# VectorE rounds the fill's operands with one-element maxima in place of copies, and the turning of -max and 1/sum moves one step later

## The chip, the cores and the metric

The kernel runs on one core of a Trainium2 chip. The metric is device time in microseconds (us), from launch to end, of one execution. A core has TensorE (PE, matmuls; PEld is its weight loading), VectorE (DVE), ScalarE (ACT), GpSimd (POOL) and SyncE (SP, which here only issues DMAs). Each engine takes its instructions strictly in the order in which they were written.

## The reference

Two independent parts, written side by side into one output of 2048 x 2048 (float32):

```python
q = (x @ wq)  -> 32 heads of 32;  k = x @ wk;  v = x @ wv     # one k, v for all heads; S = 2048, D = 1024
p = softmax(q k^T / sqrt(32));  A = concat_heads(p v) @ wo
a = xb @ hid_re^T;  b = xb @ hid_im^T                          # DFT over the hidden axis
B = seq_re @ a - seq_im @ b                                    # DFT over the sequence, real part
out = concat([A, B], axis=-1)
```

## The kernel before

**Two streams on TensorE.** The *attention* stream goes through 32 units (4 blocks of 512 queries x 8 groups of 4 heads), 32 steps to a unit, 1024 steps in all. The *fill* is every other matrix product of the kernel (q, k, v, both DFT stages, the output product), cut into groups of 128x128 by 128x512 matmuls. A fill product is made of three matmuls, high x high, high x low and low x high parts, because each operand is split into a part `hi`, rounded to float32r, and the rest `lo`. The loop over n (L753 to L766) issues one attention step and then `level` (L745) inserts as many fill matmuls as keep the fill even; in each eighth step it inserts none, since there `pv` (L674) issues 16 small matmuls of p v for each of four heads together.

**A step of attention.** `scores` (L602) has PE write a 128x1024 tile `pss` of scores (two matmuls) and DVE take its negated row maximum into `nm` (L610). `row_sums` (L613), one step behind, has ACT take exp of that tile with the maximum as bias, and its row sum into `ls`. `expo` (L665) has PE write the transposed scores `pst` of a unit that lies 44 steps back, and ACT exponentiate them into `p`. There are two buffers of `pss` and one of `pst`, so PE's next matmul into one of them waits for ACT.

**Between the two passes of a unit** the maxima and sums must be turned from columns into rows. `score_step` (L703) does it in pieces, by the number e of the step behind the unit's end: `lse_1` (e = 1), `lse_1b` (2), `lse_2` (3), all on small tiles; `lse_3` (L643, e = 5) fills up a fill group by up to five matmuls if it is near its start or end (`aside`, L378), has PE transpose -max (high and low part) and 1/sum together (`m2`, with `ident`) into a PSUM bank `psb`, and DVE copy the result to `mt`; `lse_4` (L653, e = 7) has SP send the two -max rows into the operand `qst` (two DMAs) and 1/sum to DRAM (one DMA). The transposed scores of the unit, which need these rows of `qst`, begin at e = 12. `pv` comes at e = 4, 12, 20 and 28, after that step's `score_step`. The fill's open group, the transposes and `pv` share two banks `psb` (`bank`, L328); DVE adds each `pv` result to `ov` (L685), which frees its bank.

**How a fill operand is made** (`Line`, L139): SP loads the float32 source (`r` for right operands, `m` for left ones), POOL adds further sources to it where the product needs sums (`comb`, L211), `cast` (L174) writes `hi` (`rh`, `mh`; called at L225 and L235), and `lo` (L244) has POOL write the difference (`rl`, `ml`). Each piece is issued a fixed number of fill matmuls ahead of need. `cast` is done by ACT before the fill position START (L572) and by DVE behind it. The small `CAST`s of `oh` and of `m` are other lines (L700, L638).

Of the kernel before, what the change touches and what calls it, by code (L numbers as in the profile page):

```python
# [11 lines left out]
ALU = mybir.AluOpType  # L12
AX = mybir.AxisListType
# [74 lines left out]
def tile_kernel(ctx: ExitStack, tc, xT, wq, wkv, wo, xbT, wT, cT, out):  # L88
# [3 lines left out]
    dve = Ordered(tc, nc.vector)  # L92
# [4 lines left out]
    def pool(stack, name, bufs, **kw):  # L97
        kw.setdefault("reuse_waits", "tile")
        return stack.enter_context(tc.tile_pool(name=name, bufs=bufs, **kw))
# [32 lines left out]
    op = pool(ctx, "op", 2, side="right")  # L132
# [41 lines left out]
    def cast(to, of):  # L174
        if pos["fill"] < START:
            act.activation(to, of, AF.Copy)
        else:
            dve.tensor_copy(to, of)

    def load_r(it):  # L180
        if it.pre or it.t:
# [37 lines left out]
    def hi_r(it):  # L219
        it.hi = rp.tile([P, W], F32R, name="rh")  # L220
        it.lo = rp.tile([P, W], F32R, name="rl")
        if it.pre:
            fetch(it)
        else:
            cast(it.hi, it.t[0])  # L225

    def hi_m(it):
        it.hi = mp.tile([P, 4, P], F32R, name="mh")
        it.lo = mp.tile([P, 4, P], F32R, name="ml")
        if it.pre:  # L230
            fetch(it)
            return
        _, n, w = it.t[0].shape
        it.hi, it.lo = it.hi[:, :n, :w], it.lo[:, :n, :w]
        cast(it.hi, it.t[0])  # L235
# [355 lines left out]
    def open_unit(u):  # L591
        b, g = units[u]
        assert ("q", b, g) in ready
        q = qsp.tile([P, 4, W], F32R, name="qst")
        gp.memset(q[96:P].bitcast(F32), 0.0)
        for r, src in enumerate((qh_d, ql_d, qh_d)):
            move(sp, q[r * DH:(r + 1) * DH], src[b][g].rearrange("(h d) c -> d h c", d=DH))
        qst[u] = q
        nm[u] = sm.tile([P, 2, NC], F32, name="nm")
        ls[u] = sm.tile([P, 2, NC], F32, name="ls")  # L600

    def scores(s):  # L602
        u, r = divmod(s, SU)
        i, j = divmod(r, 2)
        h, t = divmod(i, 4)
        ps = ps_s.tile([P, 2 * W], F32, name="pss")
        for a in range(2):
            k0 = (2 * j + a) * W
            te.matmul(ps[:, a * W:(a + 1) * W], qst[u][:, h, t * P:(t + 1) * P], kst[:, k0:k0 + W], start=True, stop=True)
        dve.tensor_reduce(nm[u][:, j, i:i + 1], ps, axis=AX.X, op=ALU.max, negate=True)  # L610
        pend[s] = ps

    def row_sums(s):  # L613
        if s not in pend:
            return
        ps = pend.pop(s)
        u, r = divmod(s, SU)
        i, j = divmod(r, 2)
        act.activation(ps, ps, AF.Exp, bias=nm[u][:, j, i:i + 1], accum_out=ls[u][:, j, i:i + 1])

    def lse_1(u):
        m = sm.tile([P, NC], F32, name="mm")
        d = sm.tile([P, 2, NC], F32, name="md")
        dve.tensor_tensor(m, nm[u][:, 0], nm[u][:, 1], op=ALU.min)
        for j in range(2):
            dve.tensor_sub(d[:, j], m, nm[u][:, j])
        lse[u] = m, d

    def lse_1b(u):
        act.activation(lse[u][1], lse[u][1], AF.Exp)  # L630

    def lse_2(u):
        m, d = lse[u]
        l = sm.tile([P, NC], F32, name="l")
        m2 = sm.tile([P, 3, NC], F32, name="m2")
        dve.tensor_mul(d, d, ls[u])
        dve.tensor_add(l, d[:, 0], d[:, 1])
        dve.tensor_copy(m2[:, 0].bitcast(F32R), m)  # L638
        dve.tensor_sub(m2[:, 1], m, m2[:, 0])
        dve.reciprocal(m2[:, 2], l)  # L640
        lse[u] = m2

    def lse_3(u):  # L643
        m2 = lse.pop(u)
        aside()
        pm = bank("psb")
        te.transpose(pm[:3 * NC, :P], m2.rearrange("p a b -> p (a b)"), ident)
        mt = sm.tile([3 * NC, P], F32, name="mt")
        dve.tensor_copy(mt, pm[:3 * NC, :P])
        cur["at"] += 1  # L650
        lse[u] = mt

    def lse_4(u):  # L653
        mt = lse.pop(u)
        for a in range(2):
            move(sp, qst[u][96 + a:97 + a].rearrange("o h (t c) -> o (h t) c", c=P), mt[a * NC:(a + 1) * NC])
        sp.dma_start(r_d[u], mt[2 * NC:])
# [45 lines left out]
    def score_step(s):  # L703

        if s < total:
            u, r = divmod(s, SU)
            if r == SU - 6 and u + 1 < len(units):
                open_unit(u + 1)
            scores(s)
        row_sums(s - 1)  # L710
        u, e = divmod(s - SU, SU)
        if 0 <= u < len(units):
            if e == 1:
                lse_1(u)
            elif e == 2:
                lse_1b(u)
            elif e == 3:
                lse_2(u)
            elif e == 5:
                lse_3(u)  # L720
            elif e == 7:
                lse_4(u)


# [11 lines left out]
    for s in range(SU + LEAD):  # L736
        score_step(s)
        take(7)
# [14 lines left out]
    for n in range(total):  # L753
        u, r = divmod(n, SU)
        if n == total - 12:
            w1 = wo_set(1)
            add([o_group(NQ - 1, t, e, ws) for e, ws in ((0, w0), (1, w1)) for t in range(4)])
        score_step(n + SU + LEAD)
        if ends:
            ends.pop(0)()  # L760
        expo(n)
        if r == 16:
            inverse(u)
        if r % 8 == 0 and n:
            pv(*divmod(n // 8 - 1, 4))
        level(n)  # L766
# [72 lines left out]
```

## Time and profile before

| what | value |
|---|---|
| median of 3 runs (lowest to highest) | 2849.58 us (2846.28 to 2852.26) |
| the profiled execution's own time | 2849.53 us |
| its span, first to last instruction | 2847.8 us |
| granted TensorE clock, mean | 0.997 |
| busy PE, ACT, DVE, POOL | 98%, 77%, 68%, 43% of the span |

The profiled execution's time is 1.7 us over its span, and 0.05 us under the median of the runs. In the profile's lines, a group is `line engine operation out<-in shapes xcount | busy us, mean ns of one | idle time just before them <- what ended it`. Nearly every instruction passes through one helper, so the line is L66 throughout and tiles tell the groups apart. The ends of matmuls are modelled: in the trace a 128x512 matmul lasts 0.39 us while the next one starts 0.23 us after it, so a PE that shows as busy can still be waiting a little.

### The profile page before, as it was taken

Reading aid. Unit: us, or ns where it says so; the run is one execution under the profiler, and the core shown is the slowest. Engines: PE = TensorE matmul, PEld = TensorE weight load, DVE = VectorE, ACT = ScalarE, POOL = GpSimd, SP = SyncE. Lnnn points to the kernel's source line nnn. Section 1 sums busy time; section 2 is a strip of 40 time slices with the busy share of each in tenths; the row PEclk is TensorE's granted clock in tenths of the full one; section 3 lists DMA queues with packets and bytes.
Section 4 is the critical chain, followed back from the end, with each engine's and each line's share of the span. In section 5 each row is a group of like instructions: output and inputs, shape, how many; then the busy total and the mean of one; then the engine's idle time right before and its main releaser. Section 6 shows DMA issues by size and latency. Waiting matters only on the chain.

```text
span 2847.8 us, 39945 instructions
## 1 busy us (share of the span) xinstructions
PE 2794.1 (98%) x13904; PEld 1929.8 (68%) x13904; DVE 1948.0 (68%) x2430; ACT 2185.7 (77%) x3151; POOL 1212.5 (43%) x928
## 2 busy tenths in 40 slices
PE   7999999999999999999999999999999999999999
PEld 5776676767666767676767666666666666667656
DVE  6876677777777777776777677677777676766511
ACT  4578788878787888888888888778788788888740
POOL 1211123454324346555664455766666753520000
PEclk9999999999999999999999999999999999999999
DMA  8865425765576455554552454654555533554445
GB/s 295 294 198 172 149 101 167 237 213 197 193 233 212 163 178 160 154 169 123 170 175 93 134 156 133 200 172 138 176 167 155 174 113 100 160 155 138 126 141 170
DMA packets 315722, 480.83 MB, mean 169 GB/s; under 512 B 33408, under 2 KB 98432, under 8 KB 315520
## 3 DMA queue, kind: packets, MB, share of 16 engines
q1 hardware_dynamic: 315520, 478.28, 52.8%
q8 instruction: 109, 1.79, 0.3%
q14 instruction: 93, 0.76, 0.1%
HBM read 364.12 MB, written 112.98 MB: 168 GB/s over the span
## 4 chain that ended last, share of the span: by engine, by line
PE 83%; DVE 7%; ACT 3%; DMA 3%; issue 2%; POOL 1%; SPq 1%; POOLq 0%; ACTq 0%; DVEq 0%
PE psb L66 53%; PE pss L66 15%; PE pst L66 15%; DVE nm L66 2%; ACT pss L66 1%; ACT p L66 1%; DMA ql<-ql 1%; DVE mh L66 1%; DVE rh L66 1%; DVE ov L66 1%; SPq L66 1%; POOL m L66 0%; DMA r<-s 0%; POOL ml L66 0%; DVE md L66 0%
## 5 line engine op out<-in xcount | busy, mean ns | idle before, releaser
L66 DVE TENSOR_REDUCE nm<-pss 128x1 f32<-128x1024 f32 x1024 | 1248.5, 1221 | 379.4 <-PE pss L66 376.6
L66 ACT ACTIVATE p<-pst 128x1024 f32<-128x1024 f32 x1024 | 1051.9, 1027 | 429.4 <-PE pst L66 426.5
L66 ACT ACTIVATE pss<-pss,nm 128x1024 f32<-128x1024 f32 x1024 | 1113.9, 1088 | 149.1 <-DVE nm L66 142.2
L66 PE MATMUL psb<-rh,mh 128*128 128x512 f32 (+1 forms) x1852 | 731.6, 395 | 12.0 <-ACT rh L66 8.2
L66 PE MATMUL psb<-rh,ml 128*128 128x512 f32 (+1 forms) x1852 | 731.9, 395 | 0.7 <-POOL ml L66 0.7
L66 PE MATMUL psb<-rl,mh 128*128 128x512 f32 (+1 forms) x1852 | 729.9, 394 | 0.3 <-DVE rl L66 0.3
L66 PE MATMUL pss<-kst,qst 128*128 128x512 f32 x2048 | 658.6, 403 | 17.2 <-ACT pss L66 16.6
L66 PE MATMUL pst<-qst,kst 128*128 128x512 f32 x2048 | 659.7, 403 | 10.2 <-ACT p L66 9.2
L66 POOL TENSOR_TENSOR rl<-r,rh 128x512 fp32r<-128x512 f32 x214 | 281.9, 1318 | 736.3 <-DVE rh L66 537.8
L66 POOL TENSOR_TENSOR ml<-m,mh 128x512 fp32r<-128x512 f32 x292 | 383.8, 1315 | 484.4 <-DVE mh L66 247.0
L66 PEld LDWEIGHTS pss<-kst,qst 128*128 128x128 f32 x2048 | 373.0, 188 | 208.2 <-issue 93.9
L66 PE MATMUL psb<-p,v 128*32 128x512 f32 x4096 | 466.5, 596 | 0.6 <-DVE h L66 0.5
L66 PEld LDWEIGHTS pst<-qst,kst 128*128 128x128 f32 x2048 | 372.7, 189 | 136.2 <-ACT p L66 54.5
L66 PEld LDWEIGHTS psb<-rh,mh 128*128 128x128 f32 (+1 forms) x1852 | 347.6, 188 | 97.5 <-ACT rh L66 8.7
L66 PEld LDWEIGHTS psb<-rh,ml 128*128 128x128 f32 (+1 forms) x1852 | 347.6, 188 | 84.1 <-POOL ml L66 1.1
L66 PEld LDWEIGHTS psb<-rl,mh 128*128 128x128 f32 (+1 forms) x1852 | 347.3, 188 | 84.5 <-DVE rl L66 1.6
L66 PEld LDWEIGHTS psb<-p,v 128*32 128x32 f32 x4096 | 120.2, 110 | 277.3 <-issue 258.0
L66 POOL TENSOR_TENSOR m<-m,m 128x512 f32<-128x512 f32 x192 | 252.6, 1316 | 13.2 <-DMA m<-in_cT_dram 7.8
L66 DVE TENSOR_TENSOR ov<-ov,psb 128x512 f32<-128x512 f32 x96 | 66.0, 688 | 265.9 <-PE psb L66 265.7
L66 POOL TENSOR_TENSOR r<-r,r 128x512 f32<-128x512 f32 x112 | 149.0, 1331 | 199.1 <-DMA r<-in_wT_dram 101.7
L66 ACT ACTIVATION_READ_ACCUMULATOR pss<-pss,nm 128x1 f32 x1024 | 208.6, 204 | 0.0
L66 DVE CAST mh<-m 128x512 fp32r<-128x512 f32 x291 | 167.1, 574 | 17.5 <-POOL m L66 10.6
(68 smaller groups left out, 848.6 us busy)
## 6 DMA issues: line engine op xcount, KB each, us to landing
m<-in_cT_dram SPq DMA_DIRECT2D x384, 256.0 KB, 3.7
r<-s SPq DMA_DIRECT2D x192, 256.0 KB, 4.3
y<-y SPq DMA_DIRECT2D x96, 256.0 KB, 4.4
r<-in_wT_dram SPq DMA_DIRECT2D x80, 256.0 KB, 3.8
m<-in_xbT_dram SPq DMA_DIRECT2D x80, 256.0 KB, 4.2
y<-u SPq DMA_DIRECT2D x80, 256.0 KB, 2.9
qst<-qh SPq DMA_DIRECT2D x64, 256.0 KB, 5.5
s<-y SPq DMA_DIRECT2D x64, 256.0 KB, 3.5
```

The lines of the kernel that those rows point to most:

```text
L66: return lambda *a, **k: self.tc.keep_in_program_order(f(*a, **k))
```

## The change

`cast` on DVE, behind START, becomes a maximum over a last axis of one element, with the same 128x512 numbers in and out; the output type float32r does the rounding as before. The condition of L175 and ACT's branch stay. `lse_3` goes from e = 5 to e = 6, `lse_4` from e = 7 to e = 8.

```diff
         if pos["fill"] < START:
             act.activation(to, of, AF.Copy)
         else:
-            dve.tensor_copy(to, of)
+            dve.tensor_reduce(to.rearrange('p a b -> p (a b)').unsqueeze(2) if len(to.shape) == 3 else to.unsqueeze(2), of.rearrange('p a b -> p (a b)').unsqueeze(2) if len(to.shape) == 3 else of.unsqueeze(2), axis=AX.X, op=ALU.max)
...
                 lse_2(u)
-            elif e == 5:
+            elif e == 6:
                 lse_3(u)
-            elif e == 7:
+            elif e == 8:
                 lse_4(u)
```

## The prediction

> **What bounds the kernel now.** I read the page first: engines, then the chain of work that ended last.
>
> ```profile
> span 2847.8 us, 39945 instructions
> PE 2794.1 (98%) x13904; PEld 1929.8 (68%) x13904; DVE 1948.0 (68%) x2430; ACT 2185.7 (77%) x3151; POOL 1212.5 (43%) x928
> PE 83%; DVE 7%; ACT 3%; DMA 3%; issue 2%; POOL 1%; SPq 1%; POOLq 0%; ACTq 0%; DVEq 0%
> ```
>
> PE is the bound. No matmul is added or taken away, so only what PE loses by waiting can change: 53.7 us show as idle (2847.8 - 2794.1). Next the waits, longest totals of PE and of what feeds it (us, times, longest).
>
> ```profile
> ACT pss L66 <- DVE nm L66: 142.2, 129, 20.0
> PEld pst L66 <- ACT p L66: 54.5, 127, 1.9
> PEld pss L66 <- ACT pss L66: 36.8, 44, 4.7
> PE pss L66 <- ACT pss L66: 16.6, 13, 4.2
> PEld psb L66 <- DVE ov L66: 13.7, 22, 1.6
> PE pst L66 <- ACT p L66: 9.2, 34, 1.5
> ```
>
> ACT waits for DVE's row maximum `nm`, and PE then waits for ACT to give back a score tile. Behind that stands the rounding on DVE. First its groups of the view by line and shape (count | busy us, mean ns of one | idle before), with an ordinary DVE subtraction of the same size and one of its lse_1 operations beside it; then, from the views by tile, the durations (min/median/max, ns).
>
> ```profile
> L66 DVE CAST mh<-m 128x512 fp32r<-128x512 f32 x291 | 167.1, 574 | 17.5 <-POOL m L66 10.6
> L66 DVE CAST rh<-r 128x512 fp32r<-128x512 f32 x214 | 123.1, 575 | 24.6 <-PE pss L66 14.6 <-DMA r<-in_wo_dram 7.2 <-DMA r<-in_xT_dram 2.9
> L66 DVE TENSOR_REDUCE nm<-pss 128x1 f32<-128x1024 f32 x1024 | 1248.5, 1221 | 379.4 <-PE pss L66 376.6
> L66 DVE TENSOR_TENSOR rl<-h,rh 128x512 fp32r<-128x512 f32 x8 | 5.0, 672 | 0.0
> L66 DVE COPY h<-psb 128x512 f32<-128x512 f32 x56 | 38.3, 684 | 3.4 <-PE psb L66 3.3
> ```
>
> ```profile
> L66 DVE CAST mh<-m x291: 355/419/1542, 47.9 to 2493.4; 128x512 fp32r<-128x512 f32 x146
> L66 DVE CAST rh<-r x214: 362/419/2110, 51.2 to 2813.2; 128x512 fp32r<-128x512 f32 x107
> L66 DVE TENSOR_REDUCE nm<-pss x1024: 1155/1225/1229, 65.6 to 2689.8; 128x1 f32<-128x1024 f32 x171
> L66 DVE TENSOR_TENSOR md<-mm,nm x64: 159/174/1323, 141.3 to 2692.3; 128x16 f32<-128x16 f32 x64
> ```
>
> A cast takes 419 ns at the median, yet 574 on average, and up to 2110. The same 512 elements cannot need that. What a long one is doing is seen in the timeline (start us, us, what; in brackets the idle time before it), for DVE, POOL, ACT and PE in turn.
>
> ```profile
> 1811.14 1.50 DVE L66 CAST mh<-m 128x512 fp32r<-128x512 f32 x1 [0.99 <-POOL m L66]
> 1812.57 1.52 DVE L66 CAST rh<-r 128x512 fp32r<-128x512 f32 x1
> 1814.00 2.34 DVE L66 TENSOR_REDUCE nm<-pss 128x1 f32<-128x1024 f32 x2
> ```
>
> ```profile
> 1811.07 1.29 POOL L66 TENSOR_TENSOR ml<-m,mh 128x512 fp32r<-128x512 f32 x1
> 1812.32 1.48 POOL L66 TENSOR_TENSOR r<-r,r 128x512 f32<-128x512 f32 x1
> ```
>
> ```profile
> 1815.31 1.09 ACT L66 ACTIVATE pss<-pss,nm 128x1024 f32<-128x1024 f32 x1 [2.80 <-DVE nm L66]
> ```
>
> ```profile
> 1814.06 0.39 PE L66 MATMUL psb<-rh,mh 128*128 128x512 f32 x1
> 1814.28 0.39 PE L66 MATMUL psb<-rl,mh 128*128 128x512 f32 x1
> 1816.57 0.73 PE L66 MATMUL pss<-kst,qst 128*128 128x512 f32 x2 [1.90 <-ACT pss L66]
> ```
>
> Each cast began just after a POOL operation had begun and ended 0.3 us after it: 1811.07 + 1.29 = 1812.36 against 1812.64, 1812.32 + 1.48 = 1813.80 against 1814.09. So a cast that finds POOL at work is held until POOL is done. Two holds in a row, DVE 2.2 us late, ACT idle 2.80 us, PE idle 1.90. The row maximum, which reads PSUM, is never held (1229 at most).
>
> **The change part by part: the rounding.** What it removes: the holds, 291 x (574 - 419) + 214 x (575 - 419) ns = 45 + 33 = 78 us of DVE. What it adds: a slower operation. No row has a maximum over single elements, out of SBUF and with 512 results. From below it costs what an unheld cast does, 0.419 us; from above what the 1024-element maximum does, 1.221 us, if every result took two cycles. The nearest rows, 512 elements in one pass on DVE, say 0.672 and 0.684; I take 0.68. DVE then has 505 x (0.68 - 0.574) = 53 us more to do, 2001 us of 2848, 70%.
>
> What the holds cost PE now: by the waits above it idles 16.6 + 9.2 = 25.8 us for ACT. A matmul's end is modelled 0.16 us late (0.39 long, the next about 0.23 later), so each of the 127 + 44 waits that the weight loads show hides up to 0.16 more: 27 us. Together some 53. In the quoted case the change moves DVE from 1814.09 to 1811.14 + 2 x 0.68 - 0.07 = 1812.43 (neighbours on DVE overlap by 0.07: 1811.14 + 1.50 against 1812.57), 1.65 us earlier, and gives PE 1.65 of its 1.90 + 0.16, 80%; the rest is DVE's wait for POOL's sum `m`, which stays. Not all waits have a cast behind them: lse_1's operations with two SBUF inputs are held as well (`md`: median 174, up to 1323 ns) and remain so. I put the casts' part at six tenths. 53 x 0.8 x 0.6 = **26 us gained** (bounds: 0 and 53).
>
> The Trainium skill, "SBUF — State Buffer", section "Who interferes with whom", tells of such a hold as an exclusive port pair shared by VectorE and GpSimd: copies and casts in a two-port mode take it for a whole instruction, and tensor_reduce on trn2 never does. The quoted holds agree with the first half; of the second the trace shows only maxima out of PSUM. By the page the gain above stands; if an SBUF-reading maximum were held like a cast, the sum would be that of the third rival.
>
> What the longer unheld cast costs: between two maxima of a light step DVE has little room.
>
> ```profile
> 1301.07 1.23 DVE L66 TENSOR_REDUCE nm<-pss 128x1 f32<-128x1024 f32 x1 [0.19 <-PE pss L66]
> 1303.16 1.23 DVE L66 TENSOR_REDUCE nm<-pss 128x1 f32<-128x1024 f32 x1 [0.86 <-PE pss L66]
> 1301.54 1.03 ACT L66 ACTIVATE p<-pst 128x1024 f32<-128x1024 f32 x1
> 1302.46 1.09 ACT L66 ACTIVATE pss<-pss,nm 128x1024 f32<-128x1024 f32 x1
> 1302.96 0.63 PE L66 MATMUL pst<-qst,kst 128*128 128x512 f32 x2
> ```
>
> The room is 1303.16 - 1302.30 = 0.86 us. One cast of 0.68 fits; two end 2 x 0.68 - 0.07 - 0.86 = 0.43 late. ACT has 0.16 of slack behind the maximum (1302.30 to 1302.46), PE 0.39 behind ACT (1302.57 to 1302.96), so a pair is absorbed (0.43 < 0.55), and only a pair beside a third DVE operation reaches PE. There is a cast in half of the 1024 steps on average; if every second `rh` fell beside an `mh`, 107 pairs, ACT would be late by 107 x 0.27 = 29 us in all, of which I let a tenth through: **3 us lost** (bounds 0 and 29). POOL's `lo` starts 0.26 us later behind an unheld cast; its lead of several fill matmuls hides that.
>
> **The turning.** `lse_3` comes in the step right behind a `pv`, and its transposes take the bank that `pv` has just used. PE, PEld and DVE of one such step, by the timeline:
>
> ```profile
> 2043.22 0.73 PE L66 MATMUL pss<-kst,qst 128*128 128x512 f32 x2
> 2044.10 0.29 PE L66 MATMUL psb<-ident,m 128*48 128x128 f32 x1
> ```
>
> ```profile
> 2044.09 0.10 PEld L66 LDWEIGHTS psb<-ident,m 128*48 128x48 f32 x1 [0.58 <-DVE ov L66]
> ```
>
> ```profile
> 2043.36 0.69 DVE L66 TENSOR_TENSOR ov<-ov,psb 128x512 f32<-128x512 f32 x1
> ```
>
> The addition ends at 2044.05 and the transpose follows. The second `pss` matmul starts by 2043.56 (it is 0.39 long, ending 2043.95, for the usual form), so the gap is 0.54 where 0.23 would do: 0.31 us, in 22 waits, **7 us gained** (bounds: 0, and the 13.7 us that the weight loads show). One step later, over 2 us on, the addition is long done. `aside` and the copy to `mt` move along: the same matmuls in another order, and a copy behind a maximum as before. What could be late next is `lse_4`: its three DMAs leave SP a step later. In this unit:
>
> ```profile
> 2045.43 1.16 SPq L66 DMA_DIRECT2D qst<-mt  x2
> 2060.36 0.73 PE L66 MATMUL pst<-qst,kst 128*128 128x512 f32 x2 [0.18 <-ACT p L66]
> DMA to landing us min/median/max: 1.6/1.8/3.2
> ```
>
> From issue to the first use are 14.9 us; both rows have landed by 0.58 + 3.2 = 3.8 at worst. A step less (2.1 to 2.9 us) leaves 8 us: nothing on PE's path. Queued behind them on SP are loads due many matmuls later, and 1/sum is read only 16 steps into the next pass.
>
> **Sum**, against the profiled execution's own 2849.5 us (2847.8 span and 1.7 around it; the median of the runs is the same): -26 + 3 - 7 = -30, **2820 us**, 1.1% less. With the choices a third off either way: 2806 to 2834.
>
> **Rivals.**
> 1. *More comes back.* POOL's operation beside a held cast took 1.48 in place of 1.29 us; without holds POOL's sums, on which casts wait, are earlier too, and eight tenths of all 53 us return: 2849.5 - 42 - 7 = 2800. For it: DVE's idle 0.99 us for POOL in the quoted hold. Against: lse_1's holds stay.
> 2. *The holds were covered.* ACT is 77% busy, and what DVE loses ACT might make up before PE asks; then only the turning counts: 2849.5 - 7 = 2842.5. Against: PE's own 1.90 us in the quoted case.
> 3. *The lost rate decides, slower.* The maximum runs at one element a cycle, and is held or not held without PE's waits changing; the pairs make ACT late, and ACT, not PE, sets the light steps, which at 2.09 us (1301.07 to 1303.16) just hold its 1.09 + 1.03. All 29 us arrive: 2849.5 - 7 + 29 = 2871. It decides as soon as a pair ends more than 0.16 us past the room of 0.86. Against: ACT idles 23% of the span. The Trainium skill, "VectorE: DVE Perf Modes", section "Rules for kernel authors", warns of just this: a tensor_reduce runs at the base rate and is the slowest operation, where a float32 copy within SBUF runs at twice it; its fixed 150 cycles would make (512 + 150) / 0.96 = 690 ns, an estimate from that page. By that alone nothing would be gained; the trace's 574 ns average says that the doubled rate is mostly lost already.
> 4. *Single-element maxima take two cycles, slower.* At 1.22 us a lone cast is 1.22 - 0.07 - 0.86 = 0.29 late, absorbed; a pair is 1.51 late, 0.96 past ACT's and PE's slack, x 107 = 103: 2849.5 - 26 - 7 + 103 = 2920. It decides from about 0.9 us for one, where the 107 pairs eat the 33 us. For it: no row excludes it. Against: every other 512-element row is under 0.70.
> 5. *The rows of `qst` land late:* PE waiting at each unit's start; with 8 us to spare hardly.
>
> **How the numbers follow.** Forecast 0.56, rival 1 0.12, rival 2 0.14, rival 3 0.08, rival 4 0.08, rival 5 0.02. A measurement of this kernel can tell about 0.2% (5.7 us) from no change; rival 2 lies at that edge and is halved. Faster: 0.56 + 0.12 + 0.07 = 0.75; same 0.07; slower 0.18. The range reaches from rival 1's 2800, with 4 us for its own spread, over rival 2 and up to 2858, and leaves out the rest of the slower cases.
>
> **What would show it.** A group of 505 maxima `mh`, `rh` near 0.68 us, minimum and maximum close together; the 419 ns CASTs gone; ACT's wait for `nm` down from 142 towards 80 us; PE's idle 53.7 us towards 35; POOL's mean durations lower; PEld's wait for `ov` near 0; no wait of PE for `qst<-mt`. Wrong would be: maxima above 0.9 us, or held ones; ACT's wait for `nm` as long as now; a new wait at the transposes.

## The result, and the profile after

The changed kernel takes 2841.81 us (median of 8 runs, 2840.23 to 2843.98), the kernel before 2850.27 in the same measurement (8 runs, 2846.28 to 2853.23). The ratio is 0.9972, 95% interval 0.9961 to 0.9983: faster by 8 us, not by the 30 that were forecast. Differences in us below are differences of such ratios times 2850; each ratio has about 0.0012 to either side, so a difference between two kernels is good to some 5 us.

The page of the changed kernel: span, engines, and the chain that ended last by engine.

```profile
span 2838.8 us, 39953 instructions
PE 2789.2 (98%) x13904; PEld 1926.1 (68%) x13904; DVE 1993.5 (70%) x2430; ACT 2184.6 (77%) x3151; POOL 1191.7 (42%) x928
PE 80%; DVE 7%; DMA 3%; issue 3%; POOL 2%; ACT 2%; SPq 1%; POOLq 0%; ACTq 0%; DVEq 0%
```

DVE has 45.5 us more to do, POOL 21 less. PE's idle is 2838.8 - 2789.2 = 49.6 us, where 53.7 were before and 35 were expected. The roundings themselves came out as forecast, by shape and by tile (last the minimum, median and maximum in ns):

```profile
L66 DVE TENSOR_REDUCE mh<-m 128x512 fp32r<-128x512 f32 x291 | 196.4, 675 | 24.4 <-POOL m L66 16.4 <-DMA m<-in_wq_dram 7.0 <-DMA wq<-mh 0.9
L66 DVE TENSOR_REDUCE rh<-r 128x512 fp32r<-128x512 f32 x214 | 144.5, 675 | 25.8 <-PE pss L66 14.3 <-DMA r<-in_wo_dram 7.6 <-DMA r<-in_xT_dram 2.0
```

```profile
L66 DVE TENSOR_REDUCE mh<-m x291: 622/676/689, 48.1 to 2484.9; 128x512 fp32r<-128x512 f32 x146
```

0.675 us on average, never above 0.689: nothing holds them. What that does is seen at a pair of roundings that was held in the kernel before, in the same way as the pair that the prediction quotes. There, on DVE, ACT and PE:

```profile
2260.48 1.49 DVE L66 CAST mh<-m 128x512 fp32r<-128x512 f32 x1 [0.95 <-POOL m L66]
2263.33 2.34 DVE L66 TENSOR_REDUCE nm<-pss 128x1 f32<-128x1024 f32 x2
2264.64 1.09 ACT L66 ACTIVATE pss<-pss,nm 128x1024 f32<-128x1024 f32 x1 [2.75 <-DVE nm L66]
2265.89 0.78 PE L66 MATMUL pss<-kst,qst 128*128 128x512 f32 x2 [1.84 <-ACT pss L66]
```

The same pair in the changed kernel, on DVE, POOL, ACT and PE (`mh` waits 0.95 us for POOL's sum as before, `rh` follows):

```profile
2255.41 0.69 DVE L66 TENSOR_REDUCE mh<-m 128x512 fp32r<-128x512 f32 x1 [0.95 <-POOL m L66]
2256.01 0.68 DVE L66 TENSOR_REDUCE rh<-r 128x512 fp32r<-128x512 f32 x1
2256.60 2.35 DVE L66 TENSOR_REDUCE nm<-pss 128x1 f32<-128x1024 f32 x2
```

```profile
2255.33 1.30 POOL L66 TENSOR_TENSOR ml<-m,mh 128x512 fp32r<-128x512 f32 x1
2256.58 1.30 POOL L66 TENSOR_TENSOR r<-r,r 128x512 f32<-128x512 f32 x1
```

```profile
2257.91 1.09 ACT L66 ACTIVATE pss<-pss,nm 128x1024 f32<-128x1024 f32 x1 [0.87 <-DVE nm L66]
```

```profile
2259.17 0.73 PE L66 MATMUL pss<-kst,qst 128*128 128x512 f32 x2
2260.09 0.73 PE L66 MATMUL pst<-qst,kst 128*128 128x512 f32 x2 [0.18 <-ACT p L66]
```

POOL works through beside DVE. From the first rounding to the first maximum are 2256.60 - 2255.41 = 1.19 us, against 2263.33 - 2260.48 = 2.85 before; ACT waits 0.87 in place of 2.75 us, PE 0.18 in place of 1.84. In this place the working of the prediction holds. The pair that the prediction itself quotes came out otherwise. In the changed kernel it begins here (DVE, POOL, ACT):

```profile
1816.62 0.69 DVE L66 TENSOR_REDUCE mh<-m 128x512 fp32r<-128x512 f32 x1 [2.43 <-POOL m L66]
1812.30 3.04 POOL L66 TENSOR_TENSOR y<-y,h 128x512 f32<-128x512 f32 x2 [5.38 <-DMA r<-s]
1818.53 1.09 ACT L66 ACTIVATE pss<-pss,nm 128x1024 f32<-128x1024 f32 x1 [2.35 <-DVE nm L66]
```

No hold is left, but DVE waits 2.43 us for POOL's sum `m`, which stands behind two other sums, and ACT 2.35 in place of 2.80 us. (With the copies kept and the turning moved, in e1 below, DVE waits 2.43 us at this pair too, so the maximum did not bring this wait.) The waits as a whole hardly moved:

```profile
DVE nm L66 <- PE pss L66: 328.4, 513, 2.0
ACT pss L66 <- DVE nm L66: 138.5, 146, 20.6
PEld pst L66 <- ACT p L66: 58.8, 146, 2.0
PEld pss L66 <- ACT pss L66: 32.3, 47, 4.7
PE pss L66 <- ACT pss L66: 10.1, 12, 4.3
PE pst L66 <- ACT p L66: 9.6, 33, 1.6
PE psb L66 <- DVE ql L66: 4.3, 3, 1.6
PE psb L66 <- DVE h L66: 4.2, 4, 1.1
```

ACT still waits 138.5 us for the row maximum (142.2 before), now 146 times in place of 129: fewer long waits, more short ones. Three rows of before, to set beside the first and the last two:

```profile
DVE nm L66 <- PE pss L66: 376.6, 576, 1.9
PE psb L66 <- DVE ql L66: 2.4, 2, 2.0
PE psb L66 <- DVE h L66: 0.5, 1, 0.5
```

The list counts waits of over 0.15 us. In 576 of 1024 steps DVE stood idle that long until PE had the scores; in most of the other 448 it was still busy with something else when they came. With the longer roundings there are 513 and 511. The last two rows, in which PE's fill groups wait for DVE to empty a bank, have grown from 2.9 to 8.5 us.

### The profile page after: what moved, and what is told of

Read it like the earlier page. It is cut to its first block, busy times and chain, and to the rows that moved or that the text cites. A ratio compares the mean times of both kernels' runs of the same rounds, so it can differ in the third digit from the quotient of the medians.

```text
span 2838.8 us, 39953 instructions
## 1 busy us (share of the span) xinstructions
PE 2789.2 (98%) x13904; PEld 1926.1 (68%) x13904; DVE 1993.5 (70%) x2430; ACT 2184.6 (77%) x3151; POOL 1191.7 (42%) x928
## 4 chain that ended last, share of the span: by engine, by line
PE 80%; DVE 7%; DMA 3%; issue 3%; POOL 2%; ACT 2%; SPq 1%; POOLq 0%; ACTq 0%; DVEq 0%
PE psb L66 51%; PE pss L66 15%; PE pst L66 14%; DVE nm L66 3%; ACT pss L66 1%; ACT p L66 1%; DMA r<-s 1%; POOL ml L66 1%; POOL m L66 1%; SPq L66 1%; DVE mh L66 1%; DVE rh L66 0%; DMA m<-in_cT_dram 0%; DVE md L66 0%; POOL rl L66 0%
## 5 line engine op out<-in xcount | busy, mean ns | idle before, releaser
L66 ACT ACTIVATE pss<-pss,nm 128x1024 f32<-128x1024 f32 x1024 | 1113.5, 1087 | 145.8 <-DVE nm L66 138.5
L66 PE MATMUL pss<-kst,qst 128*128 128x512 f32 x2048 | 658.6, 402 | 10.4 <-ACT pss L66 10.1
L66 POOL TENSOR_TENSOR ml<-m,mh 128x512 fp32r<-128x512 f32 x292 | 377.3, 1293 | 509.4 <-DVE mh L66 247.6
L66 PEld LDWEIGHTS pst<-qst,kst 128*128 128x128 f32 x2048 | 369.9, 188 | 142.2 <-ACT p L66 58.8
L66 DVE TENSOR_REDUCE mh<-m 128x512 fp32r<-128x512 f32 x291 | 196.4, 675 | 24.4 <-POOL m L66 16.4
```

The costliest lines, as they stand in the source:

```text
L66: return lambda *a, **k: self.tc.keep_in_program_order(f(*a, **k))
```

## The experiments

Four kernels take the change apart. Theory A: the holds were worth what the prediction says, and the length of the unheld rounding ate it. Its rivals are in the texts on record. All go on from the changed kernel, which turns at e = 6 and 8.

**e1, the turning alone.**

```diff
-            dve.tensor_reduce(...)      # the one-element maximum
+            dve.tensor_copy(to, of)
```

> The copies stay, only the turning moves one step later. Theory A (the turning gave its 7 us, and in the rounding the longer maxima ate what the vanished holds gave): about 2842.5 us, 0.9974 of before, no PEld wait for ov at the transposes, holds as before. Rival B (the turning's gain was lost again by the reordered matmuls, and the rounding gave the whole): 2850, ratio 1.000. Rival C (both parts gain, the forecast's way, at half size): about 2846.

2845.73 us, ratio 0.9986 (0.9978 to 0.9995): 4 us gained, as rival C says. **e2, the maxima alone.**

```diff
-            elif e == 6:   # lse_3
+            elif e == 5:
-            elif e == 8:   # lse_4
+            elif e == 7:
```

> Maxima in place of the copies, the turning where it was. Theory A: about 2849.5, within 0.1% of before, since 78 us of holds go and 505 x 0.256 = 129 us of length come. Rival B: about 2842. Rival C: about 2846.

2844.83 us, ratio 0.9981 (0.9972 to 0.9990): 5.4 us, rival C again. The parts add up (9.4 against 8), and theory A's "nothing from the rounding" is wrong by these 5 us. **e3, as long as the maximum, but held like the copy**, since it reads two operands from SBUF.

```diff
-            dve.tensor_reduce(...)
+            dve.tensor_tensor(to, of, of, op=ALU.max)
```

> The rounding as a maximum of the source with itself, two SBUF inputs, turning moved: as long as the one-element maximum when free (0.675 us), but held by POOL as the copy is. It prices the holds alone, against the changed kernel. Theory A: holds are worth about 20 us or more, so 2862 or above. Rival D (holds never reached PE, they were covered): 2842, as the changed kernel, although its DVE operations show means near 0.83 us.

2870.29 us, ratio 1.0073 (1.0061 to 1.0086). The groups by shape and two waits of this kernel:

```profile
L66 DVE TENSOR_TENSOR mh<-m 128x512 fp32r<-128x512 f32 x291 | 251.8, 865 | 22.3 <-POOL m L66 13.2 <-DMA m<-in_wq_dram 9.1
L66 DVE TENSOR_TENSOR rh<-r 128x512 fp32r<-128x512 f32 x214 | 175.2, 819 | 24.1 <-PE pss L66 14.3 <-DMA r<-in_wo_dram 6.8 <-PE psb L66 1.7
```

```profile
ACT pss L66 <- DVE nm L66: 190.0, 176, 20.9
PE pss L66 <- ACT pss L66: 26.7, 30, 3.8
```

Above 675 ns it is held 291 x 190 + 214 x 144 ns = 86 us, much as the copy was (78). Against e1 it differs by the length of a free rounding, 1.0073 - 0.9986 = 0.0087, **25 us for the length**; against the changed kernel by the holds, 1.0073 - 0.9972 = 0.0101, **29 us for the holds**. Both take the way over `nm`, ACT and `pss`: ACT's wait is 190 us. Rival D is out. Each price was taken beside the other, though: the 25 us are the length of a rounding that is held as well, the 29 us the holds of one that is already long. A short rounding that nothing holds was not run. **e4, the length alone**, doubled by reading each element twice.

```diff
-            dve.tensor_reduce(t.unsqueeze(2), o.unsqueeze(2), ...)
+            dve.tensor_reduce(t.unsqueeze(2), o.unsqueeze(2).to_broadcast([P, W, 2]), ...)
```

> A maximum over two copies of each element (a stride of zero), turning moved: no holds, 1.21 us in place of 0.675. It prices the length alone. Theory A: length is dear once a second operation stands between two row maxima; 0.54 us more on 505 roundings cost at least as much per us as the first 0.256 did (about 20 us), so 2880 or above. Rival D (DVE has room): under 2850.

2942.42 us, ratio 1.0322 (1.0307 to 1.0336): 0.0350, 100 us more than the changed kernel. One group and one wait:

```profile
L66 DVE TENSOR_REDUCE mh<-m 128x512 fp32r<-128x1024 f32 x291 | 351.4, 1208 | 17.9 <-POOL m L66 12.0 <-DMA m<-in_wq_dram 4.2 <-POOL ml L66 1.4
```

```profile
DVE nm L66 <- PE pss L66: 218.4, 300, 2.0
```

505 x (1.208 - 0.675) = 269 us of DVE cost 100 of PE, 0.37 each, and no hold is in play (none takes over 1.223 us); the first 505 x 0.256 = 129 us, beside the holds of e3, cost 25, 0.19 each. Length is not free in either range. DVE now waits for the scores in only 300 of 1024 steps.

The next four ask which lateness of DVE counts. **e5, the maximum only for operands that POOL has summed.**

```diff
-    def cast(to, of):
+    def cast(to, of, summed):            # called with len(it.srcs) > 1
...
-        else:
+        elif not summed:
+            dve.tensor_copy(to, of)
+        else:
```

> The changed kernel, but operands with a single source are copied again and only those that POOL has summed go through the maximum. The first four runs priced the holds at about 29 us and the length at about 25. Theory A (a hold strikes a rounding that waits for POOL's sum, since POOL goes straight on to its next operation; so these have most of the holds, and the single-source ones only pay for the length): faster than the changed kernel, about 2835. Rival F (holds strike whatever comes while POOL is busy, and POOL is busy in the same stretches): no gain, 2842 to 2848.

2839.10 us, ratio 0.9961 (0.9947 to 0.9975), 3 us below the changed kernel: inside the uncertainty, so neither theory is told apart. **e6, fewer small operations that POOL can hold.**

```diff
-        dve.tensor_tensor(m, nm[u][:, 0], nm[u][:, 1], op=ALU.min)
-        for j in range(2):
-            dve.tensor_sub(d[:, j], m, nm[u][:, j])
+        dve.tensor_reduce(m.unsqueeze(2), nm[u].rearrange('p j c -> p c j'), axis=AX.X, op=ALU.min)
+        dve.tensor_sub(d, m.unsqueeze(1).to_broadcast([P, 2, NC]), nm[u])
...
-        dve.tensor_add(l, d[:, 0], d[:, 1])
-        dve.tensor_copy(m2[:, 0].bitcast(F32R), m)
+        dve.tensor_reduce(l.unsqueeze(2), d.rearrange('p j c -> p c j'), axis=AX.X, op=ALU.add)
+        dve.tensor_reduce(m2[:, 0].bitcast(F32R).unsqueeze(2), m.unsqueeze(2), axis=AX.X, op=ALU.max)
```

> The changed kernel with lse_1 and lse_2 written with fewer operations that POOL can hold: minimum and sum of the two halves, and the rounding of -max, as maxima, minima and sums over a last axis (one input), and the two subtractions as one. Theory A (holds on DVE cost PE about 0.37 us for each us of hold, as 29 for 78, whatever operation is held): these small ones were held some 25 us in the changed kernel, so about 10 us faster, 2832. Rival G (small operations stand where DVE has room): 2842.

2828.30 us, ratio 0.9923 (0.9910 to 0.9935): 14 us below the changed kernel. The first two of the replaced operations in the changed kernel, and in e6:

```profile
L66 DVE TENSOR_TENSOR mm<-nm 128x16 f32<-128x16 f32 x32 | 14.4, 449 | 0.0
L66 DVE TENSOR_TENSOR l<-md 128x16 f32<-128x16 f32 x32 | 13.7, 428 | 1.1
```

```profile
L66 DVE TENSOR_REDUCE mm<-nm 128x16 f32<-128x32 f32 x32 | 5.7, 177 | 0.0
L66 DVE TENSOR_REDUCE l<-md 128x16 f32<-128x32 f32 x32 | 6.0, 188 | 1.1
```

The minimum of 16 and 16 elements took 449 ns on average, with a median of 170 and up to 1305, as POOL held some of them; as a reduction it takes 177, at most 180. DVE's busy time falls from 1993.5 to 1970.1 us, by shorter holds for the most part and by one subtraction less, and these 23 us are worth 14. That is 0.6 each, more than the roundings' holds (29 for 86); perhaps because the small operations stand in a row before the next row maximum, which was not tried. Theory A's direction holds, rival G is out. **e7, no finishing of a fill group ahead of the transposes.**

```diff
-        aside()
+        aside(False)                     # in aside: elif finish and j > g.n - 6
```

> The changed kernel, but lse_3 no longer finishes a fill group that is near its end before the transposes. In the turning-only run the transposes' wait went, but PE's first matmul of a fill group waited some 8 us for DVE to empty the bank (h, ql, y). Theory H (the transposes take the free bank, so the next group must have the bank that has just been filled): these waits go, about 2835. Rival I (the next group then waits for the copy to mt instead): 2842.

2844.42 us, ratio 0.9972 (0.9962 to 0.9983): no change. Of its waits:

```profile
PE psb L66 <- DVE mt L66: 3.0, 6, 0.7
PE psb L66 <- DVE ql L66: 1.7, 1, 1.7
```

The waits for `h` and `ql` mostly go, and one for `mt` comes, as rival I says; two banks between three users leave one of them waiting. **e8, at most one rounding in a step.**

```diff
+                    if k == 2 and pos["s"] and not self.items[self.n[k]].pre:
+                        if pos["s"] > 1:
+                            break
+                        pos["s"] = 2
                     self.step(k)         # in pump; score_step sets pos["s"] = 1, the tail sets 0
```

> The changed kernel, but at most one rounding is issued in an attention step unless a matmul needs it now. Theory A (the length costs because roundings come in pairs, or beside another DVE operation, between two row maxima, and 0.86 us hold only one): faster, about 2832, with ACT's wait for nm well under 138 us. Rival K (roundings beside other DVE operations cost, not pairs; or POOL's rest is late instead): 2840 or slower.

2834.36 us, ratio 0.9941 (0.9929 to 0.9954): 9 us below the changed kernel, with every rounding as long as there. Spreading the roundings is worth that much; whether it comes off the length's 25 us is not shown, as no run spreads the short copies alone. ACT's total wait hardly fell:

```profile
DVE nm L66 <- PE pss L66: 315.3, 574, 2.0
ACT pss L66 <- DVE nm L66: 134.4, 135, 20.3
```

DVE is in time in 574 steps again, as before the change, though its operations are longer. Last, both edits together, and what each part of the change is worth in that kernel. **e9, e6 and e8 together:**

> Both edits that gained: the changed kernel with the lean lse_1 and lse_2 and at most one rounding in a step. If the two gains (13.9 and 8.8 us against the changed kernel) are different lateness of DVE, they add: about 2819. If they cure the same steps: about 2826.

2822.04 us, ratio 0.9901 (0.9887 to 0.9914), the forecast's time, by another way: 20 us below the changed kernel; the gains nearly add.

```profile
ACT pss L66 <- DVE nm L66: 115.6, 126, 20.5
PEld pst L66 <- ACT p L66: 38.3, 108, 0.7
PE pss L66 <- ACT pss L66: 5.1, 6, 2.4
PE pst L66 <- ACT p L66: 3.4, 18, 0.3
```

PE's two idle rows for ACT are down from 25.8 us before to 8.5. **e10, e9 with `dve.tensor_copy` in `cast`:**

> As e9, with the copies of before in place of the maxima: what the maximum is worth once DVE has room. Theory A (with one rounding in a step the length is absorbed, so the holds' price shows bare): 12 us or more slower than e9. Rival L (holds and length weigh the same in any surrounding): 4 us slower than e9.

2828.28 us, ratio 0.9925 (0.9913 to 0.9938): 7 us slower than e9, good to some 5 us, which excludes neither theory and lies nearer to rival L's 4 than to the 12 or more of theory A. So it is not shown that spreading the roundings makes their length free. Of its copies, those of `mh` are held more than before (665 ns on average for 574), those of `rh` less (523 for 575):

```profile
L66 DVE CAST mh<-m 128x512 fp32r<-128x512 f32 x291 | 193.4, 665 | 23.2 <-POOL m L66 15.2 <-DMA m<-in_wq_dram 7.0 <-DMA wq<-mh 0.5
L66 DVE CAST rh<-r 128x512 fp32r<-128x512 f32 x214 | 112.0, 523 | 24.7 <-PE pss L66 14.6 <-DMA r<-in_wo_dram 6.1 <-DMA r<-in_xT_dram 2.3
```

At 665 ns on average the copy into `mh` gains next to nothing over the maximum's 675. **e11, e9 with the turning at e = 5 and 7:**

> As e9, with the turning at e = 5 and 7 as before: what the later turning is worth here. Theory H (the transposes' wait of 7 us turns for the most part into a fill group's wait for its bank): 2 to 5 us slower than e9. Rival B: 7 us slower.

2823.77 us, ratio 0.9909 (0.9895 to 0.9922), 2 us slower than e9, too little to be told from nothing. **e12, e9 with copies for the operands of one source:**

> As e9, with copies for the operands of a single source. Theory A (length absorbed with one rounding in a step, so single-source operands gain nothing by the shorter copy but are held again): the same as e9 or a few us slower. Rival F: 3 us faster, as in e5.

2820.09 us, ratio 0.9896 (0.9881 to 0.9911). The lowest time of all, but e9 lies inside its interval.

## Why the prediction was wrong in size

*What bounds the kernel; the holds:* right in kind. The roundings were held by POOL, the holds reached PE by `nm` and ACT, and they are gone. Their price, forecast as 26 us, is 29 by e3, for roundings that are already long. That the two numbers are so near is in part luck: the 0.8 came from one place, the six tenths were a guess, and the quoted pair got back little. The second half of the rule of the Trainium skill ("SBUF — State Buffer", section "Who interferes with whom"), that a tensor_reduce is never held, could not be seen before; the 505 maxima out of SBUF, none above 689 ns, agree with it.

*The cost of a single-element maximum:* right, 0.675 for 0.68 us; two cycles for each result (rival 4) is out.

*What the longer unheld cast costs:* this step failed. It put 3 us and e3 against e1 shows 25, near the upper bound of 29 that the same step gave and rival 3 used. The working took one light step, in which DVE had 0.86 us free, and let a tenth of its 29 us through, for pairs beside a third DVE operation. Where the loss lies can be counted in the traces of e1 (copies) and of the changed kernel (maxima, the same turning): ACT's waits for `nm`, without the first one at the start, by what DVE does between one row maximum and the next.

| DVE between two row maxima | steps | ACT's waits with copies (times, total) | with maxima |
|---|---|---|---|
| two roundings alone | 72 | 26, 33.6 us | 6, 4.7 us |
| two beside another operation | 27 | 8, 9.5 us | 22, 19.1 us |
| one alone | 157 | 20, 16.5 us | 18, 15.5 us |
| one beside another operation | 135 | 35, 32.2 us | 46, 34.8 us |
| no rounding | 632 | 44, 37.7 us | 53, 43.8 us |

A pair alone is absorbed, as the prediction said, and there ACT gets back 29 us of waiting. Beside another operation a pair is not, and neither is many a single rounding, which the working left out; these two kinds of step, and those without a rounding, lose 18 us again. (From the kernel before to e2 it is the same: 29.1 to 5.9 us at the pairs alone, 13.1 to 18.5 at those beside another operation.) So of the two terms together, 26 - 3 = 23 us, only 4 to 5 reached the time: by the prediction's own measure of PE's waits for ACT, 10.1 + 9.6 + 193 x 0.16 = 50.6 us are left of its 53. ACT's wait, which it wanted down to 80 us, stayed at 138.5, and it had named that a sign of being wrong. What the length costs a rounding that nothing holds, and so the exact split between the terms, stays open.

*The turning:* half right. PE's wait for `ov` at the transposes is gone from the list, as forecast, but e1 gained 4 of the 7 us. The prediction said of `aside` that it issues the same matmuls in another order; it did not ask which bank the next group gets. In the changed kernel, PE and DVE at one turning:

```profile
2290.92 0.27 PE L66 MATMUL psb<-ident,m 128*48 128x128 f32 x1
2292.76 0.49 PE L66 MATMUL psb<-rh,mh 128*128 128x512 f32 x1 [1.11 <-DVE h L66]
```

```profile
2290.89 1.23 DVE L66 TENSOR_REDUCE nm<-pss 128x1 f32<-128x1024 f32 x1 [0.50 <-PE pss L66]
2292.03 0.68 DVE L66 TENSOR_TENSOR h<-h,psb 128x512 f32<-128x512 f32 x1
```

A fill group ends just ahead of the transposes, these take the other bank, and the next group must have the one whose emptying (`h`) stands behind a row maximum on DVE. PE idles 1.11 us: rarer than the old wait, but longer. In e1 `ql` and `h` hold PE for

```profile
PE psb L66 <- DVE ql L66: 4.8, 3, 2.0
PE psb L66 <- DVE h L66: 3.7, 4, 1.1
```

which is 8.5 us where it was 2.9 before, and the 5.6 more are most of the 7 that the transposes' wait was put at. So the 4 us that e1 measures are what is left of two opposite terms, and with an interval of 1 to 6 us their sizes stay open. The DMAs to `qst` had time enough, as expected; no wait of PE for them is listed.

*The sum:* 4 us for the rounding (the changed kernel against e1; 5.4 by e2) and 4 for the turning, 8 in all, where 26 - 3 and 7 were put. That 29 - 25 is 4 as well proves nothing, since both are taken from e3.

## What to carry to other kernels

An operation that trades speed for freedom from another engine's hold moves two terms, and each must be priced on the whole run: the holds by the excess of mean over median, the longer free operation by what else its engine has to do before the next operation that others wait for. One light step does not show that; count how often the operation stands alone, in a pair, and beside another one. The mere number of steps in which the engine is late does not price it either: e6 and e10 take 2828 us each, with 524 and 574 waits of DVE for the scores. Then spread the work and look for small operations that are held for far longer than they run; here both together brought 20 us on top of the change's 8. When something is moved past a buffer's user, follow which buffer the next user is left with.

## What the runs showed of the hardware

- A maximum over one element out of SBUF, 512 results, takes 0.675 us, and over two elements (the same one read twice) 1.208: the time goes by elements read, not by results.
- A copy on DVE that begins while POOL runs an operation waits for that operation's end. In the kernel before, 98 of the 505 roundings took over 0.55 us; each of them began beside a POOL operation and ended 0.28 to 0.29 us after it, 0.13 less than a free copy takes.
- A DVE operation with two SBUF inputs is held by POOL's sums and differences too: 865 and 819 ns on average for a median of 683 and 684 (e3). By POOL's memset of `qst`, which only writes, it is not: 14 roundings of e3 began with 0.2 us or more of a memset to go, and none took over 0.685 us; of the copies before, 10 began so, and they took 0.63 to 2.11 us.
- Small operations are held for far longer than they run. Additions and minima of 128x16 averaged 428 and 449 ns, where the same numbers as a one-input reduction took 188 and 177.
